# A mixer kernel: the first weight block of a projection multiplied chunk by chunk over seven row blocks instead of row block by row block

## The chip, the cores and the metric

One core of one Trainium2 chip runs the kernel. The metric is the device time of one execution in microseconds (us); a smaller number is better. Where the profile and this text name engines: PE is TensorE's matmul, PEld its weight load, DVE is VectorE, ACT is ScalarE, POOL is GpSimd, SP is SyncE, which here only issues DMAs. ACTq, SPq and POOLq are the DMA-issuing parts of ACT, SP and POOL.

## The reference

All of it is float32, with S = 2048 positions and D = 640 channels. An attention branch `a` and a spectral branch `b` of the same input `x` are mixed by a gate `g` per position.

```
g = _sigmoid((x * gate_w).sum(-1, keepdims=True))
qkv = (x @ wqkv).reshape(B, S, 3, 32, 20)             # 32 heads of 20 channels
# each position attends to itself and to 7 positions, 2, 4, ... 14 before it
attn = softmax(einsum(q, gathered k) * 20**-0.5, masked below 0)
a = einsum(attn, gathered v).reshape(B, S, D) @ wo
b = irfft2(rfft2(x) * (w_r + 1j * w_i), s=(S, D))
return g * a + (1 - g) * b
```

What is changed is a piece of `x @ wqkv`, together with the gate's sum.

## The kernel before, in words

**Tiling.** The 2048 positions are 16 row blocks of 128, block j holding positions p*16 + j. The 640 channels that are summed over are five chunks of 128 (t = 0 to 4). The columns of `wqkv` are four weight blocks hg of 480 columns; block 0 carries two more, one of them the gate's weights, so it has 482. `qkv(par, hg)` (L707) multiplies the eight row blocks of one parity, j = 2*jj + par, with one weight block; eight such units, u = 4*par + hg, make up the projection. Unit 0 is even row blocks by weight block 0, and it is the first real work of the program.

**A product in three.** For speed each float32 operand is split into a high part, rounded to the type float32r by a cast (`xe` for positions, `w` for weights, by ACT), and a low part, the rest (`tensor_sub`, DVE or POOL). One chunk of one row block is then three matmuls: high x by high w, high x by low w, low x by high w. The table `WHOLE` (L1136) lists (row block, chunk) pairs of unit 0 that are instead one matmul in plain float32, straight from the raw tiles, which needs no split. On PE each float32 matmul shows as two records of the trace. Before, `WHOLE` holds all five chunks of row block 0.

**The start.** `work` (L569) first multiplies a dummy tile six times (`warm`). `load_x` (L682) for block 0 issues the raw positions in two pieces and between them, by `load_chunk` (L678), the five chunks of weight block 0, those with even t from ACT, those with odd t from SP. All raw data goes to staging tiles `st`. `load_w` (L657) splits the weights; the other seven even row blocks follow one by one as DMAs of 128 x 640 from SP, each with a cast on ACT and a subtraction on DVE. After them SP loads the raw chunks of weight block 1 (`raw<-in_wqkv`) and the rows of `x` for the spectral branch (`fx<-in_x`), which DVE folds (`fold`, L826).

**PSUM.** Every matmul group of a row block writes one bank. `BP` (L27) is a ring of seven banks, and the eighth holds copies of q. A bank is read by ACT into one half of an `ev` tile (L726), the gate's column into `z` (L728), and each pair of row blocks goes to DRAM by a DMA from ACT's queue (L735). There are two `ev` tiles, so a third pair waits until the first pair's DMA has landed.

**Who sets the order.** The code only records its operations (`Plan.record`). `Plan.order` (L277) then places them on the five engines with a list scheduler and its own cost table, repeats that with disturbed priorities drawn from a random generator started with `SEED` (L298, L302 to L309), and keeps the best by its model; the instructions are issued engine by engine in that order (`issue`, L464), and each engine takes them in it. DMAs from SP and ACT take eight completion semaphores (DMAHW0 to DMAHW7) in turn, in program order. A DMA whose semaphore is still in use by the one eight before it waits for that one's landing, and what stands behind it on the issuing engine waits too. Neither this nor the loading of ACT's function table, which stands ahead of ACT's first arithmetic instruction, is in the planner's cost table (`cost`, L242).

**After the projection.** Attention (`attend`, L745) runs on DVE, POOL and ACT beside the projection; the spectral branch (`freq`, L871) follows the last unit on PE and exchanges halves of a tile by DMA (`P<-X`), which POOL then multiplies; last come the output projections (`project_even`, `project_odd`) and the inverse transform (`spatial`).

Of the kernel before, what the change touches and what calls it, by code (L numbers as in the profile page):

```python
# [13 lines left out]
F32 = mybir.dt.float32  # L14
# [3 lines left out]
NJ = 16  # L18
# [3 lines left out]
HC = 80  # L22
ROWS = 7 + 1024
# [3 lines left out]
BP = (0, 1, 2, 3, 4, 5, 6)  # L27
# [440 lines left out]
                exec(*op.call)  # L468


TURNS, AGAIN, MOVE, SEED = 6, 60, 2.0, 0
DRAWS, SOONEST, LATER_BY = 3, 2.4, 0.6
ENGS = ("PE", "DVE", "ACT", "POOL", "SP")
RATE = 380e3
# [11 lines left out]
def staged(gens, n):  # L486
    for step in range(len(gens) + n - 1):
        for i in range(max(0, step - n + 1), min(step, len(gens) - 1) + 1):
            next(gens[i], None)


class Ring:
# [5 lines left out]
    def next(self, name, *shape, dtype=F32):  # L498
        self.turn += 1
        tag = self.tags[(self.turn - 1) % len(self.tags)]  # L500
        return self.pool.tile([128, *shape], dtype, tag=tag, name=name, bufs=1)


class Mixer:
# [64 lines left out]
    def work(self):  # L569
        p, ins = self.p, self.ins  # L570
        S = p.sp
        self.xT, self.wh, self.wl, self.folded = {}, {}, {}, {}
        self.xraw, self.wraw = {}, {}
        self.warm()
        xe = self.one("xe", 8, 2, 5, 128, dtype=F32R, tag="big")
        st = [t[:, i] for t in (self.xr.next(f"st{i}", 2, 641) for i in range(7)) for i in range(2)]
        self.load_x(st, xe[:, 0], 0)
        self.load_w(st, 0)
        for j in range(2, NJ, 2):
            self.load_x(st, xe[:, j // 2], j)  # L580
        self.xr.turn = 0
        S.dma_start(self.fc, ins["t_fc"][:, 0:128])
        self.zero_rows()
        self.qkv(0, 0)
        self.load_w(None, 1)
        for q in range(8):
            self.fold(q)
        self.qkv(0, 1)
        self.load_w(None, 2)
        self.qkv(0, 2)  # L590
        self.load_w(None, 3)
        for j in range(1, NJ, 2):
            self.load_x(None, self.xr.next(f"xo{j}", 2, 5, 128, dtype=F32R), j)
        self.qkv(0, 3)
        self.zg = self.one("zg", 5, NJ, 128, tag="big")
        for hg in (3, 2, 1, 0):
            self.qkv(1, hg)
            if hg:
                self.load_w(None, hg - 1)
                for q in {3: (0, 1), 2: (2, 3), 1: (4, 5, 6, 7)}[hg]:  # L600
                    self.cols(q)
                    if q < 6:
                        self.load_f(q + 2)
        self.sign = self.one("sign", 1)
# [12 lines left out]
        for _ in range(5):
            for a in pair:
                next(a, None)
        p.chain = ""  # L620
        freq = [self.freq(g) for g in GORD]
        staged(freq, 4)
        p.chain = "even"
        for j in range(0, NJ, 2):
            self.project_even(j)
        p.chain = ""
        staged([self.spatial(j) for j in range(1, NJ, 2)], 2)
        staged([self.spatial(j) for j in range(0, NJ, 2)], 3)
        odd = [self.project_odd(j) for j in range(1, NJ, 2)]
        next(odd[0])  # L630
        for this, later in zip(odd, odd[1:] + [iter(())]):
            next(later, None)
            next(this, None)
# [41 lines left out]
            (p.pool if hg != 1 and st is None and (hg, t, 1 in self.xT) not in W_DVE else p.dve).tensor_sub(lo[t], raw, hi[t].bitcast(F32))  # L675
            p.chain = ""

    def load_chunk(self, place, hg, t):  # L678
        raw = self.wraw[hg, t] = place[:, 0:482]
        (self.p.act if t % 2 == 0 else self.p.sp).dma_start(raw, self.ins["w0"][t])  # L680

    def load_x(self, st, pair, j):  # L682
        p = self.p
        hi, lo = self.xT[j] = [pair[:, i].rearrange("p t a -> p (t a)") for i in range(2)]
        raw = (self.rawr.next(f"xt{j}", 640) if st is None else st.pop(0))[:, 0:640]
        self.xraw[j] = raw
        src = self.ins["xT"][j].rearrange("p t a -> p (t a)")
        p.chain = "" if j else "first"
        if j:
            p.sp.dma_start(raw, src)  # L690
        else:
            for c0, c1, chunks in ((0, 128, (0,)), (128, 640, (2, 1, 4, 3))):
                p.sp.dma_start(raw[:, c0:c1], src[:, c0:c1])
                for t in chunks:
                    self.load_chunk(st.pop(0), 0, t)
        p.chain = "x" if st is None else ""
        (p.act.copy if j else p.dve.tensor_copy)(hi, raw)
        if st is None and j in XO_DVE:
            for c in (0, 320):
                b = self.ps(BP, f"xs{j}_{c}")[:, 0:320]  # L700
                p.act.copy(b, raw[:, c : c + 320])
                p.dve.tensor_sub(lo[:, c : c + 320], b, hi[:, c : c + 320].bitcast(F32))
        else:
            (p.pool if st is None else p.dve).tensor_sub(lo, raw, hi.bitcast(F32))
        p.chain = ""

    def qkv(self, par, hg):  # L707
        p, d = self.p, self.qkv_d
        n = 482 if hg == 0 else 480
        u = 4 * par + hg  # L710
        for jj in range(8):
            j = 2 * jj + par
            hi, lo = self.xT[j]
            b = self.ps(BP, f"qkv{u}_{jj}")
            terms = []
            for t in (0, 2, 1, 4, 3) if u + jj == 0 else range(5):
                x = slice(128 * t, 128 * t + 128)
                if u == 0 and (jj, t) in WHOLE:
                    terms.append((self.xraw[j][:, x], self.wraw[hg, t]))
                else:  # L720
                    terms += [(a[:, x], w[hg][t]) for a, w in ((hi, self.wh), (hi, self.wl), (lo, self.wh))]
            for i, (a, w) in enumerate(terms):
                p.pe.matmul(b[:, 0:n], a, w, start=(i == 0), stop=(i == len(terms) - 1))
            if jj % 2 == 0:
                ev = self.evr.next(f"ev{u}_{jj}", 6, 2, HC)
            p.act.copy(ev[:, :, jj % 2], b[:, 0:480].rearrange("p (i c) -> p i c", i=6))  # L726
            if hg == 0:
                p.act.copy(self.z[:, j : j + 1], b[:, 480:481])  # L728
            if jj % 2:
                to = bass.AP(  # L730
                    tensor=d.tensor,
                    offset=d.offset + (6 * u * ROWS + 7 + jj - 1) * HC,
                    ap=[[8 * HC, 128], [ROWS * HC, 6], [1, 2 * HC]],
                )
                p.act.dma_start(to, ev.rearrange("p i j c -> p i (j c)"))  # L735

    def gates(self):
        p = self.p
# [394 lines left out]
WA, WB, WC = ("w0", "w1", "w2", "w3", "w4"), ("w5", "w6", "w7", "w0", "w1"), ("w2", "w3", "w4", "e0", "e1")  # L1133
WPLACES = WA + WB + WC + WB + WC + WB + ("w2", "w3", "w4", "e1", "w5")

WHOLE = tuple((0, t) for t in range(5))  # L1136
ODD_POOL = ()
XO_DVE = ()
W_DVE = ()
FOLD_DVE = tuple(range(8))  # L1140

# [23 lines left out]
def weights_of(g, wr, wi):  # L1165
    up, down = rows_of(g)
    return (up, wr), (up, wi), (down, wi), (down, wr)


def arrays_of(inputs):  # L1170
    x, wqkv, wo, wr, wi, gw = (
        np.asarray(inputs[k]) for k in ("A_x", "A_wqkv", "A_wo", "B_w_r", "B_w_i", "gate_w")
    )
    xj = x.reshape(128, NJ, D)
    w = wqkv.reshape(5, 128, 3, 4, GC).transpose(3, 0, 1, 2, 4).reshape(4, 5, 128, 480)
    a = {
        "x": np.concatenate([xj, xj[:, :, :1]], 2),
        "xT": xj.transpose(1, 2, 0).reshape(NJ, 5, 128, 128).transpose(0, 2, 1, 3),
        "w0": np.concatenate([w[0], gw.reshape(5, 128, 1), np.zeros((5, 128, 1), np.float32)], 2),
        "wqkv": w[1:],  # L1180
        "wo": wo.reshape(5, 128, D),
        "ws": np.stack([np.stack([w[r][:, PERM] for r, w in weights_of(g, wr, wi)], 1) for g in range(16)]),
    }
    a = {k: np.ascontiguousarray(v) for k, v in a.items()}
    a.update(dft_tables())
    return a
# [15 lines left out]
```

## Time and profile before

| | us |
|---|---|
| median of 3 runs | 462.2 (462.19 to 463.9) |
| the profiled execution | 462.63 |
| its span, first to last instruction | 460.9 |
| PE busy | 448.6 |
| DVE busy | 416.4 |
| POOL busy | 324.3 |
| ACT busy | 210.0 |

The profile is of one execution; its span is 1.7 us shorter than the time of that execution. In a timeline row stand the start, the busy time, engine and line, operation, output <- input, shape, the count, and in brackets the idle time of the engine before it and what ended that. Nearly all rows carry L639, because the planner issues from one place; so rows are found by tile names. Buffer numbers are left out there: `xe` is the split even positions, `w` the split weights, `st` the raw staging tiles, `qkv` a bank of the projection, `ev` and `z` its copies, `qkvd` its place in DRAM.

### The profile page before, as it was taken

The page shows a single profiled execution, that of the slowest core. Times are in us where ns is not written, and L with a number is a line of the kernel's source. Part 1 is how long each engine was busy: PE and PEld are TensorE (multiplying, and loading weights), DVE is VectorE, ACT ScalarE, POOL GpSimd, SP SyncE. Part 2 cuts the span into 40 slices and gives each one's busy share as a digit, 9 for nine tenths or more (in the row PEclk, how much of TensorE's full clock was granted, in tenths as well). Part 3 has the DMA queues.
Part 4 walks back from the last instruction along what each step waited for, and adds up shares of the span by engine and source line. Part 5 has one row for each costly group of instructions (what it writes and reads, how often), then busy time and mean ns, then how long its engine had stood idle before and what let it go on. Part 6 is the DMA issues. An engine that isn't in the chain of part 4 may idle for free.

```text
span 460.9 us, 7237 instructions
## 1 busy us (share of the span) xinstructions
PE 448.6 (97%) x2465; PEld 393.6 (85%) x2465; DVE 416.4 (90%) x547; ACT 210.0 (46%) x547; POOL 324.3 (70%) x264
## 2 busy tenths in 40 slices
PE   7899999999999999999999989999999999999997
PEld 4688888888889889899887779988888999998996
DVE  4599959999999999999999999999999996989584
ACT  5432435453326454257348656656445554332120
POOL 1001644999999969999799899788787888952200
PEclk9999999999999999999999999999999999999999
DMA  8999998869697988869979998886362321546733
GB/s 297 409 367 319 390 373 269 272 190 304 174 281 227 321 260 281 263 199 295 327 216 256 295 283 240 246 280 215 115 207 74 114 70 58 165 111 197 233 110 114
DMA packets 73124, 108.53 MB, mean 235 GB/s; under 512 B 21104, under 2 KB 50800, under 8 KB 73088
## 3 DMA queue, kind: packets, MB, share of 16 engines
q1 hardware_dynamic: 40768, 69.90, 47.6%
q10 hardware_dynamic: 31408, 34.18, 23.7%
q0 software_dynamic: 912, 4.00, 2.2%
q8 instruction: 19, 0.31, 0.3%
q14 instruction: 17, 0.14, 0.1%
HBM read 72.59 MB, written 32.84 MB: 229 GB/s over the span
## 4 chain that ended last, share of the span: by engine, by line
PE 88%; DMA 4%; DVE 3%; POOL 2%; ACT 1%; issue 1%; SPq 0%; ACTq 0%; POOLq 0%; DVEq 0%
PE qkv L639 43%; PE wob L639 8%; PE woa L639 8%; PE z L639 6%; PE g L639 4%; PE ob L639 3%; PE oa L639 3%; PE v L639 3%; PE u L639 3%; PE x L639 2%; PE oTp L639 2%; DMA raw<-in_wqkv 2%; PE ha L639 2%; PE hb L639 1%; DMA st<-in_xT 1%; POOL P L639 1%
## 5 line engine op out<-in xcount | busy, mean ns | idle before, releaser
L639 PE MATMUL qkv<-w,xo 128*128 128x480 f32 (+1 forms) x480 | 107.8, 383 | 0.0
L639 PE MATMUL qkv<-w,xe 128*128 128x480 f32 (+1 forms) x465 | 102.9, 382 | 1.7 <-ACT xe L639 1.0
L639 PEld LDWEIGHTS qkv<-w,xe 128*128 128x128 f32 x465 | 87.3, 188 | 17.5 <-ACT xe L639 2.4
L639 PEld LDWEIGHTS qkv<-w,xo 128*128 128x128 f32 x480 | 89.9, 189 | 13.9
L639 ACT COPY ev<-qkv 128x480 f32<-128x480 f32 x64 | 35.5, 557 | 49.9 <-PE qkv L639 38.1
L639 PE MATMUL woa<-wo,oT 128*128 128x320 f32 x240 | 52.0, 318 | 0.0
L639 PE MATMUL wob<-wo,oT 128*128 128x320 f32 x240 | 51.5, 316 | 0.0
L639 PEld LDWEIGHTS woa<-wo,oT 128*128 128x128 f32 x240 | 39.4, 188 | 0.3
L639 PEld LDWEIGHTS wob<-wo,oT 128*128 128x128 f32 x240 | 39.2, 188 | 0.4
L639 POOL TENSOR_TENSOR P<-P,wp 128x963 f32<-128x963 f32 (+1 forms) x16 | 30.5, 1904 | 8.5 <-ACT P L639 3.7
L639 POOL TENSOR_TENSOR w<-raw,w 128x480 fp32r<-128x480 f32 (+1 forms) x20 | 25.2, 1278 | 12.6 <-ACT w L639 12.5
L639 POOL DMA_DIRECT2D fd<-fx x6 | 4.3, 717 | 39.8 <-DVE fx L639 39.8
L639 POOL TENSOR_TENSOR yi<-yi,y 128x640 f32<-128x640 f32 x8 | 12.5, 1557 | 22.1 <-DMA yi<-ad 12.9
L639 ACT CAST oT<-oTp 128x384 fp32r<-128x384 f32 (+1 forms) x32 | 13.4, 428 | 31.2 <-PE oTp L639 18.3
L639 PEld LDWEIGHTS g<-mm,s 128*128 128x128 f32 x150 | 21.4, 190 | 3.7 <-ACT zg L639 0.5
L639 PE MATMUL v<-bt,zc 128*128 128x321 f32 (+2 forms) x96 | 22.2, 347 | 1.9 <-ACT vs L639 1.0
L639 PE MATMUL oa<-gt,zg 128*128 128x161 f32 (+1 forms) x96 | 23.0, 344 | 0.0
L639 PE MATMUL g<-mm,s 128*128 128x128 f32 x150 | 22.9, 275 | 0.1
L639 PE MATMUL ob<-gt,zg 128*128 128x161 f32 (+1 forms) x96 | 22.5, 344 | 0.0
L639 PE MATMUL u<-bt,zc 128*128 128x321 f32 (+2 forms) x96 | 21.6, 344 | 0.0
L639 PEld LDWEIGHTS v<-bt,zc 128*128 128x128 f32 x96 | 16.1, 189 | 6.0 <-ACT vs L639 1.2
L639 ACT CAST w<-raw 128x480 fp32r<-128x480 f32 (+1 forms) x30 | 17.3, 592 | 8.1 <-PE qkv L639 3.3
(306 smaller groups left out, 1101.9 us busy)
## 6 DMA issues: line engine op xcount, KB each, us to landing
qkvd<-ev ACTq DMA_DIRECT2D x32, 480.0 KB, 5.7
wp<-in_ws SPq DMA_DIRECT2D x16, 642.0 KB, 4.9
raw<-in_wqkv SPq DMA_DIRECT2D x25, 240.0 KB, 7.1
fx<-in_x SPq DMA_DIRECT2D x8, 641.0 KB, 8.9
ot<-od SPq DMA_DIRECT2D x16, 320.0 KB, 3.2
fd<-fx POOLq DMA_DIRECT2D x6, 640.0 KB, 7.7
f<-fd SPq DMA_DIRECT2D x6, 640.0 KB, 6.1
P<-X ACTq DMA_DIRECT2D x16, 160.5 KB, 4.2
```

Source lines behind the costliest of these rows:

```text
L639: p.dve.memset(w, 0.0)
```

## The change

It touches unit 0 and what feeds it; the rest of the code stands as it was, but everything is ordered anew.

- Seven of the even row blocks (jj = 0 to 6) are loaded by chunk of channels instead of by row block: a new input array `xE` holds, for each chunk t, 128 channels by seven row blocks by 128 positions. Chunk 0 comes in two DMAs (row blocks 0 to 2, then 3 to 6), the others in one each, all from SP. The eighth block (jj = 7) comes as before, after them. The total of bytes is the same.
- All five weight chunks of block 0 are issued from ACT.
- The casts of a chunk of positions are two instructions, three and four row blocks wide (384 and 512 columns), all on ACT; the low parts likewise on DVE. Before there was one of 640 columns for each block, and block 0's cast was on DVE.
- `qkv_first` gives each of the seven row blocks a bank of its own and runs over chunks outside and row blocks inside. All seven banks stay open until the last chunk.
- `WHOLE` shrinks to two pairs, chunk 0 of row blocks 0 and 1. Three products go back from one float32 matmul to three matmuls each.
- `SEED` is 3 instead of 0; an empty switch, `XO_DVE`, is removed.

```
-TURNS, AGAIN, MOVE, SEED = 6, 60, 2.0, 0
+TURNS, AGAIN, MOVE, SEED = 6, 60, 2.0, 3
...
-        st = [t[:, i] for t in (self.xr.next(f"st{i}", 2, 641) for i in range(7)) for i in range(2)]
-        self.load_x(st, xe[:, 0], 0)
-        self.load_w(st, 0)
-        for j in range(2, NJ, 2):
-            self.load_x(st, xe[:, j // 2], j)
+        st = [self.xr.next(f"st{i}", 2, 641) for i in range(8)]
+        self.load_first(st, xe)
...
-        self.qkv(0, 0)
+        self.qkv_first()
...
+    def load_first(self, st, xe):
+
+        p = self.p
+        xs = [t.rearrange("p a b -> p (a b)")[:, 0:896].rearrange("p (j a) -> p j a", j=7) for t in st[0:5]]
+        place = [t[:, i] for t in st[5:8] for i in range(2)]
+        for jj in range(7):
+            self.xT[2 * jj] = [xe[:, jj, i].rearrange("p t a -> p (t a)") for i in range(2)]
+        for t in range(5):
+            p.chain = "first" if t == 0 else ""
+            self.wraw[0, t] = place[t][:, 0:482]
+            p.act.dma_start(self.wraw[0, t], self.ins["w0"][t])
+            for r0, r1 in PIECES if t == 0 else ((0, 7),):
+                p.sp.dma_start(xs[t][:, r0:r1], self.ins["xE"][t][:, r0:r1])
+        p.chain = ""
+        self.load_w(st, 0)
+        for t in range(5):
+            for r0, r1 in PIECES[::-1] if t == 0 else HALVES:
+                hi, lo = (xe[:, r0:r1, i, t] for i in range(2))
+                raw = xs[t][:, r0:r1]
+                p.act.copy(hi, raw)
+                p.dve.tensor_sub(lo, raw, hi.bitcast(F32))
+        for jj, t in WHOLE:
+            self.xraw[2 * jj, t] = xs[t][:, jj]
+        self.load_x([place[5]], xe[:, 7], NJ - 2)
+
+    def qkv_first(self):
+
+        p = self.p
+        banks = [self.ps(BP, f"qkv0_{jj}") for jj in range(7)]
+        for t in range(5):
+            x = slice(128 * t, 128 * t + 128)
+            for jj, b in enumerate(banks):
+                hi, lo = self.xT[2 * jj]
+                if (jj, t) in WHOLE:
+                    terms = [(self.xraw[2 * jj, t], self.wraw[0, t])]
+                else:
+                    terms = [(a[:, x], w[0][t]) for a, w in ((hi, self.wh), (hi, self.wl), (lo, self.wh))]
+                for i, (a, w) in enumerate(terms):
+                    p.pe.matmul(b[:, 0:482], a, w, start=(t + i == 0), stop=(t == 4 and i == len(terms) - 1), skip_group_check=True)
+        for jj, b in enumerate(banks):
+            self.store(0, 0, jj, b)
+        self.qkv(0, 0, 7)
...
-WHOLE = tuple((0, t) for t in range(5))
+WHOLE = ((0, 0), (1, 0))
+PIECES, HALVES = ((0, 3), (3, 7)), ((0, 3), (3, 7))
...
+    xT = xj.transpose(1, 2, 0).reshape(NJ, 5, 128, 128)
...
+        "xE": xT[0:14:2].transpose(1, 2, 0, 3),
```

`store` holds the old lines L724 to L735 (copy of a bank, copy of the gate's column, DMA of a pair), and `qkv` calls it.

Three places show how the order moved. The first is the beginning of ACT's queue; `st` are raw tiles, `w0_t` the split chunk t of weight block 0. Before:

```order
L639 DMA st0_85<-in_w0 128x482
L639 DMA st1_86<-in_w0 128x482
L639 DMA st2_87<-in_w0 128x482
L639 ACT_TABLE_LOAD
L639 CAST w0_0_92<-st0_85 128x482 [waits DMAHW0_49]
L639 CAST w0_2_94<-st1_86 128x482 [waits DMAHW2_49]
L639 CAST w0_4_96<-st2_87 128x482 [waits DMAHW4_49]
L639 CAST w0_1_93<-st1_86 128x482 [waits DMAHW5_49]
L639 CAST w0_3_95<-st2_87 128x482 [waits DMAHW6_49]
L639 CAST xe_84<-st3_88 128x640 [waits DMAHW7_49]
L639 CAST xe_84<-st3_88 128x640 [waits DMAHW0_49]
```

And now:

```order
L636 DMA st5_90<-in_w0 128x482 x2
L636 DMA st6_91<-in_w0 128x482 x2
L636 DMA st7_92<-in_w0 128x482 [waits DMAHW0_49]
L636 ACT_TABLE_LOAD
L636 CAST w0_0_93<-st5_90 128x482
L636 CAST xe_84<-st0_85 128x3x128 [waits DMAHW1_49]
L636 CAST w0_1_94<-st5_90 128x482 [waits DMAHW2_49]
L636 CAST xe_84<-st0_85 128x4x128 [waits DMAHW3_49]
L636 CAST w0_2_95<-st6_91 128x482 [waits DMAHW4_49]
L636 CAST xe_84<-st1_86 128x3x128 [waits DMAHW5_49]
L636 CAST xe_84<-st1_86 128x4x128
```

ACT issues five weight DMAs instead of three, and the fifth waits for semaphore DMAHW0, the one that the first weight chunk takes. The table load and the first cast stand behind it. Casts of weights and of positions now alternate.

The second place is ACT at the end of the casts of even positions, with `raw1_t` the raw chunks of weight block 1. Before:

```order
L639 COPY ev0_0_99<-qkv0_1_100 128x6x80 [waits PE_49]
L639 CAST xe_84<-st5_90 128x640 [waits DMAHW4_49]
L639 COPY z_72<-qkv0_1_100 128x1
L639 DMA qkvd_64<-ev0_0_99 128x6x160 [waits DMAHW3_49,Activation_49]
L639 CAST xe_84<-st6_91 128x640 [waits DMAHW5_49]
L639 CAST w1_0_111<-raw1_0_110 128x480 [waits DMAHW6_49]
L639 CAST w1_1_113<-raw1_1_112 128x480 [waits DMAHW7_49]
L639 CAST w1_2_115<-raw1_2_114 128x480 [waits DMAHW0_49]
```

And now:

```order
L636 CAST xe_84<-st3_88 128x4x128
L636 CAST xe_84<-st4_89 128x3x128 [waits DMAHW2_49]
L636 CAST xe_84<-st4_89 128x4x128
L636 CAST xe_84<-st7_92 128x640 [waits DMAHW3_49]
L636 CAST w1_0_112<-raw1_0_111 128x480 [waits DMAHW4_49]
L636 CAST w1_1_114<-raw1_1_113 128x480 [waits DMAHW5_49]
L636 CAST w1_2_116<-raw1_2_115 128x480 [waits DMAHW6_49]
L636 COPY ev0_0_106<-qkv0_0_99 128x6x80 [waits PE_49]
```

Copies of banks 0 and 1 and the store of that pair stood ahead of the last cast of positions, and the store had to wait for a semaphore that SP's loads also take. Now all casts of positions and three of weight block 1 stand ahead of the first copy.

The third place is PE's first matmuls after the dummy ones; `qkv0_j` is the bank of row block jj. Before:

```order
L639 MATMUL qkv0_0_98<-st0_85 128x482 [waits DMAHW3_49,DMAHW0_49]
L639 MATMUL qkv0_0_98<-st1_86,st0_85 128x482 [waits DMAHW2_49,DMAHW1_49]
L639 MATMUL qkv0_0_98<-st1_86,st0_85 128x482 [waits DMAHW5_49]
L639 MATMUL qkv0_0_98<-st2_87,st0_85 128x482 [waits DMAHW4_49]
L639 MATMUL qkv0_0_98<-st2_87,st0_85 128x482 [waits DMAHW6_49]
L639 MATMUL qkv0_1_100<-w0_0_92,xe_84 128x482 [waits Activation_49]
L639 MATMUL qkv0_1_100<-w0_0_92,xe_84 128x482 [waits DVE_49]
L639 MATMUL qkv0_2_101<-w0_0_92,xe_84 128x482 [waits Activation_49]
L639 MATMUL qkv0_1_100<-w0_0_92,xe_84 128x482 [waits DVE_49]
L639 MATMUL qkv0_1_100<-w0_1_93,xe_84 128x482 x3
```

And now:

```order
L636 MATMUL qkv0_0_99<-st5_90,st0_85 128x482 [waits DMAHW1_49,DMAHW0_49]
L636 MATMUL qkv0_2_101<-w0_0_93,xe_84 128x482 [waits Activation_49]
L636 MATMUL qkv0_2_101<-w0_0_93,xe_84 128x482 [waits DVE_49]
L636 MATMUL qkv0_1_100<-st5_90,st0_85 128x482
L636 MATMUL qkv0_2_101<-w0_0_93,xe_84 128x482 [waits DVE_49]
L636 MATMUL qkv0_3_102<-w0_0_93,xe_84 128x482 [waits Activation_49]
L636 MATMUL qkv0_3_102<-w0_0_93,xe_84 128x482
L636 MATMUL qkv0_4_103<-w0_0_93,xe_84 128x482
L636 MATMUL qkv0_3_102<-w0_0_93,xe_84 128x482 [waits DVE_49]
L636 MATMUL qkv0_4_103<-w0_0_93,xe_84 128x482 x2
L636 MATMUL qkv0_5_104<-w0_0_93,xe_84 128x482 x3
L636 MATMUL qkv0_2_101<-w0_1_94,xe_84 128x482 [waits Activation_49]
```

Before, the five float32 matmuls of row block 0 come first, each waiting only for DMAs, then row block 1 through its chunks. Now one float32 matmul comes first, then row blocks 2 to 5 with chunk 0, the second float32 matmul among them, and the second matmul of the queue waits for ACT.

More of the change, by code (lines that the diff above doesn't have):

```diff
@@ L676, in load_w @@
             p.chain = ""
-    def load_chunk(self, place, hg, t):
-        raw = self.wraw[hg, t] = place[:, 0:482]
-        (self.p.act if t % 2 == 0 else self.p.sp).dma_start(raw, self.ins["w0"][t])
+    def load_first(self, st, xe):
[37 more added lines that the diff above has]
+        self.qkv(0, 0, 7)
     def load_x(self, st, pair, j):
@@ L685, in load_x @@
         raw = (self.rawr.next(f"xt{j}", 640) if st is None else st.pop(0))[:, 0:640]
[L686 to L695, printed above, removed]
@@ L696, in load_x @@
-        p.chain = "x" if st is None else ""
[L697 to L704, printed above, removed]
+        p.sp.dma_start(raw, self.ins["xT"][j].rearrange("p t a -> p (t a)"))
@@ L705, in load_x, with qkv @@
+        p.chain = "x" if st is None else ""
+        p.act.copy(hi, raw)
+        (p.pool if st is None else p.dve).tensor_sub(lo, raw, hi.bitcast(F32))
         p.chain = ""
-    def qkv(self, par, hg):
-        p, d = self.p, self.qkv_d
+    def qkv(self, par, hg, first=0):
+        p = self.p
         n = 482 if hg == 0 else 480
         u = 4 * par + hg
-        for jj in range(8):
-            j = 2 * jj + par
-            hi, lo = self.xT[j]
+        for jj in range(first, 8):
+            hi, lo = self.xT[2 * jj + par]
@@ L714, in qkv @@
             b = self.ps(BP, f"qkv{u}_{jj}")
             terms = []
-            for t in (0, 2, 1, 4, 3) if u + jj == 0 else range(5):
+            for t in range(5):
                 x = slice(128 * t, 128 * t + 128)
[L718 to L721, printed above, removed]
+                terms += [(a[:, x], w[hg][t]) for a, w in ((hi, self.wh), (hi, self.wl), (lo, self.wh))]
@@ L722, in qkv @@
             for i, (a, w) in enumerate(terms):
                 p.pe.matmul(b[:, 0:n], a, w, start=(i == 0), stop=(i == len(terms) - 1))
[L724 to L735, printed above, removed]
+            self.store(par, hg, jj, b)
@@ new lines, in store @@
+    def store(self, par, hg, jj, b):
+        p, d = self.p, self.qkv_d
+        u, j = 4 * par + hg, 2 * jj + par
+        if jj % 2 == 0:
+            self.ev = self.evr.next(f"ev{u}_{jj}", 6, 2, HC)
+        p.act.copy(self.ev[:, :, jj % 2], b[:, 0:480].rearrange("p (i c) -> p i c", i=6))
+        if hg == 0:
+            p.act.copy(self.z[:, j : j + 1], b[:, 480:481])
+        if jj % 2:
+            to = bass.AP(
+                tensor=d.tensor,
+                offset=d.offset + (6 * u * ROWS + 7 + jj - 1) * HC,
+                ap=[[8 * HC, 128], [ROWS * HC, 6], [1, 2 * HC]],
+            )
+            p.act.dma_start(to, self.ev.rearrange("p i j c -> p i (j c)"))
@@ L1134 @@
 WPLACES = WA + WB + WC + WB + WC + WB + ("w2", "w3", "w4", "e1", "w5")
-WHOLE = tuple((0, t) for t in range(5))
+WHOLE = ((0, 0), (1, 0))
+PIECES, HALVES = ((0, 3), (3, 7)), ((0, 3), (3, 7))
 ODD_POOL = ()
-XO_DVE = ()
 W_DVE = ()
@@ L1177, in arrays_of @@
         "x": np.concatenate([xj, xj[:, :, :1]], 2),
-        "xT": xj.transpose(1, 2, 0).reshape(NJ, 5, 128, 128).transpose(0, 2, 1, 3),
+        "xT": xT.transpose(0, 2, 1, 3),
+        "xE": xT[0:14:2].transpose(1, 2, 0, 3),
         "w0": np.concatenate([w[0], gw.reshape(5, 128, 1), np.zeros((5, 128, 1), np.float32)], 2),
```

## The prediction

> **What bounds the kernel now.** I read the page first, for the busy times and the chain of work that ended last.
>
> ```profile
> span 460.9 us, 7237 instructions
> PE 448.6 (97%) x2465; PEld 393.6 (85%) x2465; DVE 416.4 (90%) x547; ACT 210.0 (46%) x547; POOL 324.3 (70%) x264
> PE 88%; DMA 4%; DVE 3%; POOL 2%; ACT 1%; issue 1%; SPq 0%; ACTq 0%; POOLq 0%; DVEq 0%
> ```
>
> PE is idle for only 12.3 us of 460.9, and 88% of the chain is PE. So a change is worth the PE idle time that it removes plus the PE work that it saves. The table by stretches shows where the idle time lies (columns: length, busy time of PE, PEld, DVE, ACT, POOL, granted clock, DMA share, GB/s).
>
> ```profile
> 4.00:8.00 4.00, 2.24 (x5) 0.97 (x6) 1.63 (x3) 1.28 (x3) 0.00 (x0) 1.00 1.00 346
> 8.00:12.00 4.00, 3.44 (x10) 1.38 (x9) 3.46 (x6) 4.00 (x9) 0.00 (x0) 1.00 1.03 398
> 20.00:24.00 4.00, 2.88 (x13) 2.12 (x13) 2.98 (x5) 3.13 (x7) 0.00 (x0) 1.00 1.02 414
> 100.00:150.00 50.00, 50.00 (x250) 43.78 (x249) 49.86 (x44) 20.01 (x53) 49.84 (x39) 1.00 0.84 251
> 250.00:300.00 50.00, 47.63 (x286) 41.07 (x285) 48.08 (x78) 32.96 (x95) 43.80 (x36) 1.00 0.87 259
> 450.00:461.00 11.00, 7.51 (x52) 7.25 (x50) 4.52 (x10) 0.00 (x0) 0.00 (x0) 1.00 0.29 112
> ```
>
> From 100 to 150 PE, DVE and POOL are all full. PE waits in the first 24 us, a little at the hand-over to the spectral branch, and at the very end. The change works on the first 24 us; PE's timeline there comes next.
>
> ```profile
> 4.85 1.05 PE L639 MATMUL qkv<-st 128*128 128x482 f32 x2 [0.86 <-DMA st<-in_xT]
> 5.74 0.97 PE L639 MATMUL qkv<-st,st 128*128 128x482 f32 x2
> 7.61 2.69 PE L639 MATMUL qkv<-st,st 128*128 128x482 f32 x6 [0.91 <-DMA st<-in_w]
> 10.17 1.13 PE L639 MATMUL qkv<-w,xe 128*128 128x482 f32 x3
> 11.86 8.20 PE L639 MATMUL qkv<-w,xe 128*128 128x482 f32 x36 [0.56 <-DVE xe L639]
> 21.04 19.14 PE L639 MATMUL qkv<-w,xe 128*128 128x482 f32 x84 [0.98 <-ACT xe L639]
> ```
>
> The weight loads beside them give the spacing of float32 records, and the chain of waits gives the long run that follows.
>
> ```profile
> 8.53 0.19 PEld L639 LDWEIGHTS qkv<-st,st 128*128 128x128 f32 x1 [0.21 <-issue]
> 8.93 0.19 PEld L639 LDWEIGHTS qkv<-st,st 128*128 128x128 f32 x1 [0.21 <-issue]
> 21.04 0.30 PEld L639 LDWEIGHTS qkv<-w,xe 128*128 128x128 f32 x2 [1.39 <-ACT xe L639]
> 21.90 118.86 PE qkv L639 x543
> ```
>
> A split matmul takes 118.86/543 = 0.219 us; a float32 record 0.40, so a float32 product 0.81 against 3 x 0.219 = 0.66 for three split ones. Up to 21.90 PE has done 10 float32 records and 3 + 36 + 2 = 41 split matmuls. Unit 0 has 5 float32 products and 35 x 3 = 105 split matmuls, so 64 are left, and its work alone would end at 21.90 + 64 x 0.219 = **35.9**. The work is 5 x 0.81 + 105 x 0.219 = 27.0; begun at 4.85, that leaves 4.0 us of waiting inside unit 0. Why PE waited at 20 stands in ACT's and DVE's timelines.
>
> ```profile
> 0.74 1.38 ACTq L639 DMA_DIRECT2D st<-in_w  x3
> 2.15 1.28 ACT L639 ACT_TABLE_LOAD   x1 [2.15 <-issue]
> 4.25 0.59 ACT L639 CAST w<-st 128x482 fp32r<-128x482 f32 x1 [0.81 <-DMA st<-in_w]
> 5.15 0.60 ACT L639 CAST w<-st 128x482 fp32r<-128x482 f32 x1 [0.31 <-DMA st<-in_w]
> 7.91 1.58 ACT L639 CAST w<-st 128x482 fp32r<-128x482 f32 x3 [2.16 <-DMA st<-in_w]
> 9.40 1.36 ACT L639 CAST xe<-st 128x640 fp32r<-128x640 f32 x2
> 19.83 0.39 ACTq L639 DMA_DIRECT2D qkvd<-ev  x1
> 20.27 0.72 ACT L639 CAST xe<-st 128x640 fp32r<-128x640 f32 x1 [3.55 <-DMA fc<-in_t_fc]
> 21.02 0.83 DVE L639 TENSOR_TENSOR xe<-st,xe 128x640 fp32r<-128x640 f32 x1 [3.51 <-ACT xe L639]
> 23.47 0.82 DVE L639 TENSOR_TENSOR fe<-fx 128x642 f32<-128x642 f32 x1
> ```
>
> The store of the first pair waited on ACT's queue for a semaphore held by a load, and the last cast of positions stood behind it: 3.55 us lost on ACT, 3.51 on DVE, and the stop of PE before 21.04.
>
> **The change, part by part.**
>
> *Float32 products.* Three become split ones: 3 x (0.81 - 0.66) = 0.45 us less PE work. The new work is 2 x 0.81 + 114 x 0.219 = 26.6 us.
>
> *The start on ACT.* The fifth weight DMA waits for the first chunk's landing, and the table load and first cast stand behind it. Landing: 4.2, where the first cast ended its wait before. Then issue 0.45 (1.38/3), load 1.28, so the cast of weights begins at 5.95 instead of 4.25. Casts of 482 columns follow each other every (1.58 - 0.59)/2 = 0.49 us; a cast of 384 takes about 0.50 by the line through 0.59 (482) and 0.72 (640). So the first positions are ready at 5.95 + 0.49 + 0.50 + 0.05 = 7.0. PE begins its one float32 product at about 4.3 to 4.8, ends it by 5.6, and then waits until 7.0, since the other float32 product stands behind the waiting matmul. That wait is the price of the fifth DMA, some 1.6 us, and all casts and, through them, all subtractions are queued behind it. Its bounds: were the load not behind it, the gain below would be 4.5; should the first chunk land only at 5.15, where the second cast ended its wait before, 1.9. I take 4.2, since the chunk is still the first DMA of its queue.
>
> On the load itself a rule and the trace differ. The load's row shows 1.28, and the cast at 4.25 began 2.10 after the load's start, still ending a wait for a DMA, so I take nothing beside it. The Trainium skill (ScalarE: Activation LUTs, What ACT_TABLE_LOAD costs) says that a load of about 1283 ns comes with about 1380 ns of drain, some 2.66 us together, which those 2.10 contradict here. By that rule the gain below would be 2.9 - 1.4 = 1.5, and the time 460.7; I give that 0.04, inside the second rival.
>
> *PE from 7.0.* Left are one float32 product and 114 split matmuls, 0.81 + 24.97 = 25.8. Are they fed? A chunk is 21 matmuls, 4.6 us of PE. It costs ACT one cast of 482 columns (0.49) and two of 384 and 512 (about 0.9 together), 1.4 us, and DVE about as much as its three subtractions have columns, 1.8 by 0.83 for 640. Data: a chunk is 482 + 896 columns, 0.71 MB, 1.8 us at the 398 GB/s of the second stretch. All three are well below 4.6, so only chunk 0 is tight; I allow 0.2. Unit 0 then ends at 7.0 + 25.8 + 0.2 = **33.0**, and the gain is 35.9 - 33.0 = **2.9 us**.
>
> *What is late next.* Weight block 1 is cast right after the positions, from 5.95 + 5 x 0.49 + 5 x 0.9 + 0.63 = 13.5 on, and PE needs it at 33. For DVE's folds and for the banks two rows of the page's DMA list count (KB each, median us from issue to landing).
>
> ```profile
> fx<-in_x SPq DMA_DIRECT2D x8, 641.0 KB, 8.9
> qkvd<-ev ACTq DMA_DIRECT2D x32, 480.0 KB, 5.7
> ```
>
> Ahead of the first `fx` stand 5 + 3 weight chunks and eight row blocks, 4.6 MB; with it 5.3 MB, landed by 17 at about 400 GB/s. So the folds, at 23.47 before, can begin near 17 to 19, and DVE gains more than PE. The first store of a pair now comes up near 22 and waits for an `fx` load that by its place in the queue lands about then, with no cast of positions behind it. Row blocks 3 to 7 all end in the last 5 us of unit 0, and the fourth pair needs the `ev` tile of the second. With 5.7 us for that store the banks of blocks 6 and 7 come free some 7 us after unit 0's end; unit 1 needs the first of them after three row blocks, 45 x 0.219 = 9.9 us. That cover is 3 us; a store that lands later than that stops PE for the difference. Changing banks from one matmul to the next costs nothing that shows: PE did so among the 84 matmuls from 21.04.
>
> *The new order elsewhere.* Everything behind is ordered anew, and the trace cannot price that. These are PE's waits at the hand-over.
>
> ```profile
> 247.45 1.08 PE L639 MATMUL v<-bt,zc 128*128 128x321 f32 x4 [0.91 <-ACT zc L639]
> 255.12 1.35 PE L639 MATMUL v<-bt,zc 128*128 128x321 f32 x6 [0.99 <-ACT vs L639]
> 268.37 1.12 PE L639 MATMUL g<-tbfirst,s 128*128 128x128 f32 x8 [1.37 <-DVE s L639]
> ```
>
> At best these 3.3 us go; most of the 3.5 after 450 is the last copy and store and stays. At worst as much comes on top. I take 0, since work and inputs there are the same.
>
> **The sum.** 462.63 (span 460.9 and 1.7 around it) - 2.9 = 459.7 for an execution like the profiled one. That lay 0.4 above the median of the runs, so I predict 462.2 - 2.9 = **459.3**.
>
> **The rivals.** A difference of 0.5%, 2.3 us, is about what a measurement of this kernel can tell from no change: under 459.9 is faster, over 464.5 slower.
>
> *More is gained.* DVE's and POOL's lead shortens the waits at the hand-over, or ACT starts earlier than I think: gain 3.8 to 6, 456.2 to 458.4. For it: DVE gains 4 us or more at its folds. Against it: POOL is as full as PE from 100 to 150.
>
> *The gain is given back.* At the hand-over PE waits for tiles that pass through POOL.
>
> ```profile
> 244.55 2.62 POOL L639 TENSOR_TENSOR pv7b<-vt7b,L7b 128x640 f32<-128x640 f32 x2
> 254.55 0.86 POOL L639 TENSOR_TENSOR wo<-wor,wo 128x320 fp32r<-128x320 f32 x1
> ```
>
> In the new order POOL has three `wo` subtractions (2.6) ahead of the end of the second group's product `P`, where one half of a `pv` (1.3) stood: 1.3 later. Such a delay at two of the three waits leaves 0.3 of the gain: 461.9. The clock belongs here too. In the stretch from 4 to 8 PE was busy for 2.24 us of 4 and the clock stayed at 1.00; were the new wait before 7.0 to halve it for the next 4 us, 2 us would go: 461.3, with 0.03. The Trainium skill (TensorE: Matmul & The Clock Gate, What's actually happening) has the clock halved after an idle window of about 3.4 us, longer than that wait.
>
> *Slower.* POOL comes to the first three groups a whole `pv` pair late each time: PE waits 3 x 2.6 = 7.8 more, 462.2 - 2.9 + 7.8 = 467.1. It decides where POOL's backlog at the first `P` exceeds what PE has left of the projection to fill with. Against it: the order puts the same pair ahead of that `P` as before, and POOL's inputs come earlier too.
>
> **Chances and range.** The forecast, 458.4 to 459.9, has 0.48; more gained 0.14; given back, 459.9 to 464.5 and mostly below 462.4, 0.30; slower 0.08. Faster is then 0.62, same 0.30, slower 0.08. From 456.8 to 462.4 lie the forecast, most of the second case and three quarters of the third, 0.8.
>
> **What would show it.** Right: ACT's table load after 4.2 and its first cast near 5.9; PE's second `qkv` matmul near 7.0 and no stop between 8 and 33; no idle time of 3.5 us on DVE before its last `xe`. Wrong: a table load before 4, PE stops between 10 and 33, a PE wait for ACT at 40 to 45, or new PE waits near 250 as large as 2.9.

## The result, and the profile after

| | us |
|---|---|
| changed, median of 20 runs | 461.4 (459.69 to 463.6) |
| before, median of 20 runs beside it | 463.88 (462.19 to 466.06) |
| ratio, with its 95% interval | 0.9942 [0.9926, 0.9958] |
| the profiled execution of the changed kernel | 463.6 (span 461.8) |

The changed kernel is 2.7 us faster [1.9, 3.4], 0.58%. The forecast difference was 2.9. Before came out 1.7 above its first three runs, and the changed kernel lies 2.1 above the forecast of 459.3 with it. The profiled execution of the changed kernel is the slowest of its 20, so its late part is looked at together with a second profile below.

The page of the changed kernel: PE's share of the span is what it was. The chain of work that ended last can't be compared, since this page follows it back over only 38% of the span.

```profile
span 461.8 us, 7229 instructions
PE 448.4 (97%) x2468; PEld 394.7 (85%) x2468; DVE 418.1 (91%) x549; ACT 209.7 (45%) x551; POOL 324.7 (70%) x264
```

The table by stretches, in the same columns as before: PE is full in the rows from 8 and from 20 us, where it was busy for 3.44 and 2.88 of 4; from 250 to 300 it has lost 1.5 us (47.63 before), in this execution.

```profile
4.00:8.00 4.00, 2.88 (x7) 1.25 (x7) 1.85 (x4) 3.31 (x5) 0.00 (x0) 1.00 1.02 375
8.00:12.00 4.00, 4.00 (x20) 3.45 (x19) 2.84 (x5) 2.43 (x5) 0.00 (x0) 1.00 1.03 410
20.00:24.00 4.00, 4.00 (x20) 3.45 (x19) 3.93 (x9) 1.46 (x7) 0.00 (x0) 1.00 1.02 417
250.00:300.00 50.00, 46.10 (x277) 39.55 (x276) 48.40 (x76) 30.88 (x89) 43.59 (x36) 1.00 0.82 260
```

PE's timeline of the start, and its waits from 240 to 290.

```profile
3.89 1.57 PE L636 MATMUL qkv<-st,st 128*128 128x482 f32 x2
6.59 0.77 PE L636 MATMUL qkv<-w,xe 128*128 128x482 f32 x2 [1.12 <-ACT xe L636]
7.19 0.97 PE L636 MATMUL qkv<-st,st 128*128 128x482 f32 x2
7.62 32.54 PE L636 MATMUL qkv<-w,xe 128*128 128x482 f32 x146
...
246.21 1.35 PE L636 MATMUL v<-bt,zc 128*128 128x321 f32 x6 [0.73 <-ACT vs L636]
253.85 1.08 PE L636 MATMUL v<-bt,zc 128*128 128x321 f32 x4 [0.99 <-ACT vs L636]
267.15 1.12 PE L636 MATMUL g<-tbfirst,s 128*128 128x128 f32 x8 [1.37 <-DVE s L636]
284.10 0.81 PE L636 MATMUL z<-ab,mm 128*128 128x321 f32 x2 [1.54 <-DVE s L636]
```

One wait is left in the start, before 6.59, and from 7.62 PE runs without a stop until 170. The wait of 1.54 at 284 is new. ACT's and DVE's timelines show the fifth weight DMA (until 4.20), the table load behind it, and DVE's first fold at 18.57, which was at 23.47.

```profile
0.74 3.46 ACTq L636 DMA_DIRECT2D st<-in_w  x5
4.23 1.28 ACT L636 ACT_TABLE_LOAD   x1 [4.23 <-DMA st<-in_w]
5.53 0.59 ACT L636 CAST w<-st 128x482 fp32r<-128x482 f32 x1
6.03 0.51 ACT L636 CAST xe<-st 128x384 fp32r<-128x384 f32 x1
...
12.91 4.03 DVE L636 TENSOR_TENSOR xe<-st,xe 128x384 fp32r<-128x384 f32 x7
...
18.57 0.82 DVE L636 TENSOR_TENSOR fe<-fx 128x642 f32<-128x642 f32 x1
```

### The profile page after: what moved, and what is told of

Its sections match the earlier page's. It is cut to its first block, busy times and chain, and to the rows that moved or that the text cites. A ratio compares the mean times of both kernels' runs of the same rounds, so it can differ in the third digit from the quotient of the medians.

```text
span 461.8 us, 7229 instructions
## 1 busy us (share of the span) xinstructions
PE 448.4 (97%) x2468; PEld 394.7 (85%) x2468; DVE 418.1 (91%) x549; ACT 209.7 (45%) x551; POOL 324.7 (70%) x264
## 5 line engine op out<-in xcount | busy, mean ns | idle before, releaser
L636 PE MATMUL qkv<-w,xo 128*128 128x480 f32 (+1 forms) x480 | 109.9, 384 | 0.0
L636 PE MATMUL qkv<-w,xe 128*128 128x480 f32 (+1 forms) x474 | 104.4, 381 | 1.1 <-ACT xe L636 1.1
L636 PEld LDWEIGHTS qkv<-w,xe 128*128 128x128 f32 x474 | 89.2, 188 | 16.7 <-ACT xe L636 2.2
L636 DVE TENSOR_TENSOR oT<-oTp,oT 128x384 fp32r<-128x384 f32 (+1 forms) x32 | 15.2, 483 | 8.4 <-ACT oT L636 8.4
```

The source lines that it names most:

```text
L636: p.dve.memset(w, 0.0)
```

## The experiments

The question was whether the 2.7 us are the start's own, or whether the order that was drawn anew behind the start makes or takes a part. For that the planner was put aside in some kernels: `issue` takes the operations in the order of a table, so that one place can be changed and the rest stays.

```
-        order = self.order()
+        order = [self.ops[int(i)] for i in ORDER.split()]
```

All differences are ratios to runs of before on the same chip, times 464 us. "Even done" is the time by which PE has done all work on even positions, from each profile; it is 114.6 before and 110.9 in the changed kernel (first `qkv<-w,xo` at 110.7, one even matmul behind it). So the start's gain, measured there, is 3.7. "Stretch" is the time from PE's first `g<-tbfirst,s` (spectral branch) to its second `woa` group (output projection), some 265 to 294, for kernels whose PE order there can be compared. Both are read from one profile of each kernel.

| kernel | even done | stretch | us against before | ratio |
|---|---|---|---|---|
| before | 114.6 | 24.7 | | |
| changed | 110.9 | 26.6 | -2.7 | 0.9942 [0.9926, 0.9958] |
| changed_again | 110.9 | 26.3 | -3.1 | 0.9933 [0.9904, 0.9961] |
| start_new_order_old | | | +1.3 | 1.0028 [0.9995, 1.0061] |
| start_new_order_old_2 | 111.4 | 24.7 | +1.5 | 1.0032 [1.0004, 1.0061] |
| start_old_order_new | 113.3 | 26.6 | -1.3 | 0.9973 [0.9953, 0.9993] |
| fifth_dma_late | 110.5 | 25.1 | -3.0 | 0.9935 [0.9914, 0.9956] |
| q5b_earlier | 112.9 | 25.9 | -3.3 | 0.9928 [0.9909, 0.9947] |
| ng_on_pool | 112.9 | 25.1 | -3.4 | 0.9926 [0.9903, 0.9948] |
| three_moves | 110.6 | 26.1 | -3.1 | 0.9933 [0.9914, 0.9953] |
| gap_filled | 110.9 | 26.5 | -3.8 | 0.9919 [0.9889, 0.9949] |
| changed_seed0 | 111.0 | | +1.4 | 1.0030 [1.0007, 1.0054] |
| before_seed3 | 115.0 | | +4.3 | 1.0093 [1.0058, 1.0128] |
| old_store_late | 113.2 | 26.3 | -1.1 | 0.9976 [0.9946, 1.0007] |

### Start and order apart

The first two kernels cross start and order: the operations of unit 0 and its loads keep the places of one kernel, all others the order of the other. A third, `changed_again`, is the changed kernel with its own order as a table.

> The changed kernel's start (every instruction of unit 0 and its loads, in its places) with everything behind it in the order of before: instructions and data are those of the changed kernel, only the engines' order behind the start differs. Theory 1, the gain of 2.7 us is the start's own (PE stops that went and three float32 products fewer): 2.2 to 3.5 us under before, and no PE stop between 8 and 32 us. Rival, the gain is the redrawn order behind the start: within 1 us of before. Third possibility, the start is worth more (unit 0 ends 3.7 us earlier in the profiles) and the new order gives some of it back: 3.3 to 4 us under before.

> The start of before with everything behind it in the changed kernel's order. Theory 1: within 1 us of before. Rival, the redrawn order makes the gain: 2.2 to 3.5 us under before. Third possibility, the new order gives back a part of the start's gain: 0.5 to 1.5 us over before.

> The changed kernel unchanged, on the same chip as the three others, for a second profile and the size of the scatter: 2.7 us under before by all theories, within 0.8. If PE's waits from 240 to 290 in the first profile are the new order's own, they come again (1.5 for DVE's s near 284, 1.4 near 267); if they belong to that one slow execution, they are smaller by half.

Both theories fell in their plain form. The new start with the old order gains nothing. The old start with the new order gains 1.3, but not behind the start: PE's timeline shows that its stop before 21.04 has gone, since ACT's store of the first pair falls on another semaphore in this order (DMAHW6, not DMAHW3) and was issued at 16.27, not at 19.83; even positions are done 1.3 earlier.

```profile
16.27 0.39 ACTq L640 DMA_DIRECT2D qkvd<-ev  x1
...
12.06 101.20 PE L640 MATMUL qkv<-w,xe 128*128 128x482 f32 x461 [0.37 <-DVE xe L640]
113.10 0.38 PE L640 MATMUL qkv<-w,xo 128*128 128x480 f32 x1
```

So the new order passes the start's gains on nearly whole (1.3 [0.3, 2.2] of 1.3, 2.7 to 3.1 of 3.7). In the first profile of the new start with the old order every matmul took twice its time over the whole execution (916.5 us), so the kernel was run once more for a profile.

> Once more the changed kernel's start with the order of before behind it, for a profile of an execution at full clock: its median was 0.3 us over before although its start is the changed one. Theory A (the start's 3.7 us is there at 110 us and is lost at the hand-over, between 240 and 300): even-position matmuls end near 110.9, PE waits of 3 us or more for ACT, DVE or DMA later. Rival B (the start itself is disturbed, since DMA semaphores and ACT's queue meet the old order badly): PE stops before 60 us, and the even-position matmuls end at 113 or later.

Theory A held, with a longest wait of 2.56 and not of 3: even positions are done at 111.4, 3.2 earlier than before, and the lead is lost at PE's later waits. Its timeline and its table by stretches of 3.4 us:

```profile
143.28 7.07 PE L637 MATMUL qkv<-w,xo 128*128 128x480 f32 x31 [1.29 <-ACT ev L637]
243.02 0.78 PE L637 MATMUL x<-ab,mm 128*128 128x321 f32 x2 [0.62 <-DVE ab L637]
246.88 1.08 PE L637 MATMUL v<-bt,zc 128*128 128x321 f32 x4 [0.91 <-ACT zc L637]
250.52 1.32 PE L637 MATMUL x<-ab,mm 128*128 128x321 f32 x2 [2.56 <-DVE ab L637]
```

```profile
247.20:250.60 3.40, 0.84 (x5) 0.49 (x4) 3.37 (x5) 0.87 (x3) 1.86 (x2) 1.00 0.58 167
250.60:254.00 3.40, 3.40 (x9) 2.60 (x10) 2.37 (x4) 1.37 (x3) 1.36 (x2) 0.50 0.15 38
254.00:257.40 3.40, 3.40 (x22) 2.87 (x22) 2.95 (x6) 2.87 (x10) 3.32 (x4) 1.00 0.96 295
```

PE waits 2.56 us for DVE, and in the 3.4 us behind that its clock is 0.50 (the column behind POOL's): 9 matmuls instead of 22, 1.7 us more. These two, 4.3 us, are more than the start's 3.2.

The mean clock that was recorded for each execution shows how far this goes: one such stretch, 3.4 us at half of 464, lowers it to 0.996. Of the 21 executions of this kernel, without the one of 916.5 us, 11 have a mean clock of 0.996 or less and take 467.3 on average; the other ten take 463.5, and before beside them 464.1. So an execution in which the clock falls is 3.8 us longer. Where it doesn't fall, only 0.6 of the start's lead is left all the same, and what takes the rest there no profile shows. None of the 30 executions of the changed kernel has a mean clock below 0.999.

### Another draw

> The changed code with SEED left at 0: the planner draws another order for the same operations. Theory 1 (the start carries the gain and the draw matters little): 2 to 3.5 us under before. Rival (the gain of 2.7 hangs on the order drawn; with the order of before behind it the same start gave 0.3 to 1.5 over before): -1 to 1.5 us under before.

> The kernel of before with SEED 3 instead of 0 and nothing else. Theory 1 (the draw matters little): within 1 us of before. Rival (a draw is worth as much as the change): 1.5 us or more under or over before; should the store of the first pair no longer stand ahead of a cast of positions, some 1.2 under, as the old start with the new order gave.

The edits are one number each.

```
-TURNS, AGAIN, MOVE, SEED = 6, 60, 2.0, 3
+TURNS, AGAIN, MOVE, SEED = 6, 60, 2.0, 0
```

The rival won both times, in the first by more than it said (1.4 over before, where it had at most 1). The changed code with seed 0 is slower than before, though its even positions are done at 111.0; before with seed 3 is slower by 4.3. In each PE waits for DVE once for over 2 us, and a stretch at half clock follows. The profile of the changed code with seed 0:

```profile
244.71 0.91 PE L636 MATMUL x<-ab,mm 128*128 128x321 f32 x2 [2.12 <-DVE ab L636]
```

```profile
241.50:245.00 3.50, 1.38 (x7) 0.98 (x7) 3.47 (x6) 2.49 (x9) 3.50 (x4) 1.00 1.06 332
245.00:248.50 3.50, 3.50 (x10) 2.48 (x9) 1.57 (x2) 1.43 (x4) 2.02 (x2) 0.53 0.40 113
```

And before with seed 3, where the stop behind the first store is 1.83 long and stands at 20.19:

```profile
20.19 2.04 PE L639 MATMUL qkv<-w,xe 128*128 128x482 f32 x8 [1.83 <-ACT xe L639]
312.39 0.92 PE L639 MATMUL g<-mm,s 128*128 128x128 f32 x4 [2.16 <-DVE s L639]
```

```profile
309.00:312.50 3.50, 1.34 (x7) 0.70 (x6) 2.55 (x4) 0.57 (x2) 3.34 (x4) 1.00 0.44 141
312.50:316.00 3.50, 3.50 (x13) 2.90 (x14) 2.06 (x6) 1.69 (x5) 3.50 (x4) 0.53 0.40 149
```

No stretch of this kind lies in the profiles of the changed kernel, whose longest wait is 1.54. With the start that the change brings, three orders thus give -2.7, +1.4 and +1.5, and `SEED = 3` is a working part of the change. Why DVE comes late in those orders was not taken apart. Nor is it shown that the wait and the half clock make the whole difference. Eleven of the 12 executions with seed 0 and five of the six of before with seed 3 have a mean clock of 0.996 or less; the one of each without it took 463.65 and 468.87. The second is as long as the others of its kernel, so there something else costs most of the 4.3.

### The store of the first pair alone

> The kernel of before with one instruction moved: ACT issues the store of the first pair behind the last cast of positions and three casts of weight block 1. Theory 1 (that store's wait of 3.55 us made PE's stop before 21.04, and the stop passes to the end): no PE stop near 20, even positions done near 113.3 instead of 114.6, and 0.8 to 1.5 us under before. Rival (what the old order behind it does at the hand-over absorbs it, as it did the changed start's 3.2): even positions done near 113.3 and a time within 0.5 of before or over it.

In the table of before, ACT's store stands one cast of positions and three casts of `w1` later.

```
-DMA qkvd<-ev
 CAST xe<-st
 CAST w1<-raw  x3
+DMA qkvd<-ev
```

```profile
11.16 102.17 PE L640 MATMUL qkv<-w,xe 128*128 128x482 f32 x465
113.17 26.15 PE L640 MATMUL qkv<-w,xo 128*128 128x480 f32 x119
```

The stop is gone and even positions are done 1.4 earlier; the time is 1.1 lower, with an interval from 2.5 lower to 0.3 higher, so that the gain passes to the end is likely and not shown. By its profile some 1.4 of the start's 3.7 is that store; the other 2.3 are, by subtraction, PE's earlier beginning (3.89 instead of 4.85), the waits before 12 us and the float32 products.

### The fifth weight DMA

> The changed kernel with one instruction moved: the fifth weight DMA stands on ACT behind the first four casts, so that ACT's table load and first cast no longer wait for the first chunk. Theory 1 (the wait's price is 1.3 to 1.6 us and PE's start passes to the end): table load near 2.8, first cast near 4.2, PE's second qkv matmul near 5.3, unit 0's end and the time 1.3 us earlier, 4 us under before. Rival, what follows the start absorbs it: the same start in the trace, and a time 2.7 under before as in the changed kernel. Second rival, the fifth chunk now lands too late and its cast stops ACT and PE near 10: time 2.7 under before or less.

```
 DMA st6<-in_w0  x2
-DMA st7<-in_w0
 ACT_TABLE_LOAD
 CAST w0_0, CAST xe, CAST w0_1, CAST xe
+DMA st7<-in_w0
```

ACT and PE begin as expected, with the first cast at 3.96 and PE's second matmul at 5.02, 1.5 earlier. But the run behind begins at 7.20 instead of 7.57 in `changed_again`, and the time is that of the changed kernel: theory 1 fell. In that profile PE's first matmuls ran at half rate (below). The same start in `three_moves`, at full rate, shows what else stands there.

```profile
4.99 0.77 PE L637 MATMUL qkv<-w,xe 128*128 128x482 f32 x2
5.60 0.97 PE L637 MATMUL qkv<-st,st 128*128 128x482 f32 x2
6.03 3.16 PE L637 MATMUL qkv<-w,xe 128*128 128x482 f32 x10
9.76 20.48 PE L637 MATMUL qkv<-w,xe 128*128 128x482 f32 x92 [0.57 <-ACT xe L637]
```

```profile
8.70 0.60 ACT L637 CAST w<-st 128x482 fp32r<-128x482 f32 x1 [1.93 <-DMA st<-in_w]
9.20 1.03 ACT L637 CAST xe<-st 128x384 fp32r<-128x384 f32 x2
```

PE runs ahead and then waits for chunk 1: its casts stand on ACT behind a weight cast that waits 1.93 for its load. The time won at the front is lost to the landings, and the price of the fifth DMA's place is 0.3 to 0.4.

### What takes back a part at the hand-over

The changed kernel's two profiles are 1.7 and 2.0 longer in the stretch from 265 to 294 than the profile of before (26.32 and 26.60 against 24.65). This compares single profiles: with the order of before behind the start, the stretch took 24.65 twice and 26.27 once (`old_store_late`). The two profiles show two different waits. In the first, `ng` (one minus the gate) took 1.92 on DVE and ended as POOL's product ended, and PE waited 1.54 for DVE at 284. In the two other profiles of this order in which `ng` was as long (1.85 in `gap_filled`, 1.90 in `start_old_order_new`) PE waited 1.47 and 1.53 at the same place. POOL and DVE in the first:

```profile
276.88 2.23 POOL L636 TENSOR_TENSOR P<-P,wp 128x963 f32<-128x963 f32 x1 [1.02 <-ACT ya L636]
277.22 1.92 DVE L636 TENSOR_SCALAR ng<-g 128x16 f32<-128x16 f32 x1
```

In the second (`changed_again`) that product began later, `ng` took 0.17, and PE's wait of 1.54 did not come again (that of 1.37 near 265 did). Here ACT stood 2.42 in front of a copy from `q5b`, a piece of q that attention reads back, whose load is issued 7.6 us later in the new order than before.

```profile
274.98 0.17 DVE L637 TENSOR_SCALAR ng<-g 128x16 f32<-128x16 f32 x1
276.37 2.27 POOL L637 TENSOR_TENSOR P<-P,wp 128x963 f32<-128x963 f32 x1 [2.74 <-ACT X L637]
281.05 0.30 ACT L637 COPY qbank<-q5b 128x160 f32<-128x160 f32 x1 [2.42 <-DMA q5b<-qkvd]
```

> The changed kernel with one instruction moved: ACT issues the load of q5b right behind the load of q4a, some 7 us earlier. In the changed kernel's second profile ACT stood 2.42 us in front of the copy from q5b, with copies for PE behind it. Theory A (part of the start's gain of 3.7 is lost to that wait): no ACT wait for q5b, and 0.4 to 1.2 us under the changed kernel, so 3.2 to 4 under before. Rival B (what PE loses between 265 and 294 hangs on DVE and POOL, above all on the ng instruction): the wait goes and the time stays within 0.4 of the changed kernel, 2.7 under before.

> The changed kernel with one instruction on another engine: ng (128x16) is worked out by POOL instead of DVE, at the same place of the order. On DVE it took 0.16 us where POOL was free, and 1.92 and 1.90 where POOL had begun a 2.23 us product 0.34 us before, ending as that product ended; behind it stand the additions that PE waits 1.54 for near 284. Theory A (DVE was held by POOL's instruction): no 1.9 us instruction on DVE near 277, no PE wait of 1.5 for DVE's s, and 0.4 to 1.2 us under the changed kernel, most in its slowest executions. Rival B (q5b's wait is the larger loss): within 0.4 of the changed kernel.

> The changed kernel with the fifth weight DMA behind four casts, the load of q5b 7 us earlier and ng on POOL, all three together. If the three losses are separate and each passes to the end: 0.4 for the start, and 0.6 to 1.5 for the other two, so 3.7 to 4.6 us under before, and PE from its first g<-tbfirst to its second woa group in 24.7 to 25.1 us, as before the change and not 26.3 to 26.6. Rival (the stretch is bound by something else): 2.7 to 3.2 under before.

The edits: the row `DMA q5b<-qkvd` some 20 rows earlier on ACT; `p.pool.tensor_scalar` for `p.dve.tensor_scalar` in `gates`; both and the later fifth DMA. Each wait went as its theory said, but the gains do not add up: with -3.3, -3.4 and -3.1 none can be told from the changed kernel. With `q5b` loaded earlier, `wp`, the spectral weights, lands later, and POOL waits for it (this is `q5b_earlier`; 4.03 in `three_moves`).

```profile
278.50 2.28 POOL L637 TENSOR_TENSOR P<-P,wp 128x963 f32<-128x963 f32 x1 [3.86 <-DMA wp<-in_ws]
```

So moving one load made the next one late. The stretch was 26.5 to 26.6 in the three profiles with a long `ng` and 25.1 to 26.3 in the five without. It was 25.1 with `ng` on POOL, though ACT still waited 1.2 for `q5b`, but also 25.1 in `fifth_dma_late`, where `ng` stayed on DVE and took 0.16. So its length differs between profiles of the same order; that `ng` costs time over many executions is not shown, and neither is how much of the start's gain this stretch takes.

### PE's rate in the first microseconds

> The changed kernel with two more dummy matmuls on PE, behind its first float32 product, where PE waits for ACT until 6.6 us; they add work and change no result. In two of six profiles with the changed start PE's matmuls took 0.44 us instead of 0.219 until 10.5 us, with a granted clock of 1.00 in the rows, and unit 0 ended 2 us later; in one until 7.0, in three not beyond 4.5. Theory A (PE runs at half rate until it has been busy for a stretch of some 3.4 us, and the wait before 6.6 spoils one such stretch): full rate by 7.1 in the profile, and a mean 0.4 to 0.8 us under the changed kernel, 3.2 to 3.6 under before, with fewer slow executions. Rival B (the switch does not hang on that wait): 2.7 to 3 under before, half rate until 10.5 in some.

The dummy matmuls stand behind the first float32 product. The rows that raised the question are from `q5b_earlier`: two split matmuls in 1.17, and 471 in 104.23.

```profile
6.74 1.17 PE L637 MATMUL qkv<-w,xe 128*128 128x482 f32 x2 [0.72 <-ACT xe L637]
7.71 1.81 PE L637 MATMUL qkv<-st,st 128*128 128x482 f32 x2
8.58 104.23 PE L637 MATMUL qkv<-w,xe 128*128 128x482 f32 x471
```

In `gap_filled`:

```profile
4.80 0.61 PE L637 MATMUL warmed<-warm 128*128 128x128 f32 x4
6.58 0.77 PE L637 MATMUL qkv<-w,xe 128*128 128x482 f32 x2 [1.17 <-ACT xe L637]
7.62 103.25 PE L637 MATMUL qkv<-w,xe 128*128 128x482 f32 x471
```

Its one profile was at full rate before the new matmuls came, so it doesn't show that they bring it. Its ratio is the lowest of all, 3.8 us under before, but its interval [-5.2, -2.4] holds the changed kernel's -2.7. This stays open. It bears on the 3.7 as well: in two of the nine profiles with the changed start that are not of the 916.5 us execution, even positions are done only at 112.9, 1.7 before the profile of before.

## Why the prediction was right

**Unit 0: right, and 0.6 too small.** Of the 146 matmuls from 7.62 on, 112 are what was left of unit 0's work, so counted back from their end it was done at 7.62 + 32.54 - 34 x 0.219 = 32.7 (33.0 was forecast). Counted in the same way, from the 84 matmuls from 21.04, before was done at 21.04 + 19.14 - 18 x 0.219 = 36.2 (35.9 in the prediction). The gain is 3.5 instead of 2.9, and 3.7 at the end of the even positions. Most of the difference is the table load: the first chunk landed by 4.2 with the fifth DMA's issue already in it, so the load began at 4.23, not 4.65. The rest lies in before, which ended later than worked out.

**The waits that go: right.** No PE stop between 8 and 33, no 3.5 us on DVE before its last `xe`, fold from 18.57 (17 to 19 forecast), no bank wait at 40 to 45.

**The table load: right.** The cast began 0.02 after the load's end (4.23 + 1.28 = 5.51, then 5.53), so the rule that I weighed, some 1.4 of drain beside the load (the Trainium skill, ScalarE: Activation LUTs, What ACT_TABLE_LOAD costs), does not hold for this one.

**The price of the fifth DMA: wrong.** "Some 1.6" is the wait, not its price: without it 0.3 to 0.4 is gained, since a weight load that chunk 1's casts stand behind lands no earlier. I had put data at 1.8 us a chunk against PE's 4.6 and held only chunk 0 to be tight.

**The new order elsewhere, "I take 0": the step that was wrong in its reason.** The three waits that bounded it came out nearly as they were (0.73, 0.99 and 1.37, against 0.91, 0.99 and 1.37). Between 111 us and the end this draw seems to lose 0.6 to 1.0 (3.7 there, 2.7 to 3.1 at the end). That is not clear of the noise, since the gain's interval reaches to 3.4 and the 3.7 is not the lead of every execution. That the forecast of 2.9 came out is thus in part luck: the start gave 0.8 more than forecast, and about as much was lost behind it, which was not forecast. The reason given, that work and inputs are the same, fell: with nearly the same operations in three other orders the time was 1.3 to 4.3 us over before, though the even positions were done 3.2 and 3.6 earlier in two of them and 0.4 later in the third. Between there and the end these lose 3.9 to 5.0, so bounds of 3.3 either way are too narrow for a draw. They priced each wait at its length, and each of the three waits of over 2 us was followed by 3.4 us at half clock, 1.7 us more.

**The rivals.** "Given back" happened at most in part, by up to 1.0; at the hand-over, loads that land late and a long `ng` were seen, and the waits behind the three `wo` subtractions did not grow. "Slower" was held to be POOL's backlog; what was seen in the slower draws is a long wait for DVE with a clock at half behind it, which is not all of the loss. I had given the clock 0.03 and looked for it before 7.0 only.

## What to carry to other kernels

When a scheduler draws the order of everything behind a change, a gain in one stage has to be measured as stage and draw apart: cross them, and time more than one draw. Ask of each wait of the busiest engine not only how long it is but whether it is long enough to slow what follows. And a wait on a queue has the price of what comes next: work that out by the landings before it is counted as a gain.

## What the runs showed of the hardware

**Half clock after a long wait.** PE's clock went to half for 3.4 us (0.50 and 0.53 in the rows) where PE had been busy for 0.84 of 3.4, 1.38 of 3.5 and 1.34 of 3.5 us (single waits of 2.56, 2.12, 2.16), and stayed at 1.00 where it had been busy for 1.86 of 3.4, with a wait of 1.54:

```profile
281.00:284.40 3.40, 1.86 (x12) 1.45 (x11) 3.30 (x6) 1.08 (x4) 2.63 (x2) 1.00 0.88 253
284.40:287.80 3.40, 3.40 (x23) 2.88 (x22) 3.40 (x5) 2.05 (x6) 2.28 (x2) 1.00 0.94 317
```

The Trainium skill (TensorE: Matmul & The Clock Gate, What's actually happening) halves the clock after an idle window of about 3.4 us; here 2.12 us of idle time in 3.5 were enough.

**A slow first 10 us.** PE's matmuls ran at half rate at the start (two split ones in 1.17 us instead of 0.77), and how long differs by profile: to under 5 us in some, to 10.5 in `q5b_earlier` and `ng_on_pool`, where even positions were done 2.0 later. The granted clock of the stretches reads 1.00 there; only the durations show it.

**An instruction held by another engine.** `ng`, 128x16, took 0.16 or 0.17 beside an idle POOL and 1.92 beside a POOL product that had begun 0.34 before it, ending with it (277.22 + 1.92 = 279.14; 276.88 + 2.23 = 279.11). It was the same in `gap_filled` (1.85) and `start_old_order_new` (1.90). That agrees with the Trainium skill (SBUF — State Buffer, Who interferes with whom): a one-input DVE instruction in a two-port mode waits until a POOL instruction that began before it is done. That `ng` ran in such a mode no profile shows.
